# Moving the transposes of a backward pass from TensorE to the DMA crossbar, with the gb factor moved into w2T and the w2 gradient

## The chip, the cores and the metric

The kernel runs on one core of one Trainium2 chip. The metric is the device time of one execution in microseconds (us), the median of several. The kernel before takes 773.13 us (3 runs, 772.19 to 773.19). A profile is one execution, whose span is some 1.75 us shorter than the time of the same run. The batches of runs went to different chips; the kernel before reads 773.2 to 773.6 us in each.

## The reference, cut to what matters

The program computes the forward pass and all gradients of one block: a spectral mixer, then an MLP with a squared ReLU. The change touches the MLP and its gradients.

```python
# S=2048 rows, D=512, F=1792; bf16
h   = layernorm(x1) * (1 + cb) + sb
r   = relu(h @ w1 + b1);  hact = r * r
out = x1 + gb * (hact @ w2 + b2)
# backward, g = grad_out:
#   gb2  = colsum(gb * g)                 gw2 = hact.T @ (gb * g)
#   gh   = 2 r * ((gb * g) @ w2.T)        gb1 = colsum(gh)
#   gw1  = h.T @ gh                       gx1 = layernorm backward of gh @ w1.T, ...
```

## The kernel before

The matmuls here contract over the 128 partitions of their operands, so several operands are needed in the other orientation. The kernel before makes each with TensorE transposes into PSUM, and ScalarE or VectorE copies the result to SBUF. I name the stages after their matmuls: C (`psH`, the first MLP matmul), D (`psO`, the second), E (`psg` and the w2 gradient), F (`psh`, the gradient through w1), G (`psw`, the w1 gradient).

```python
# D, per row tile t: gB = g*gb, transposed; w2 transposed during the first four tiles
nc.vector.tensor_tensor(gbrow, grow, modb[:, 5, :], op=ALU.mult)        # gbrow = gB[:, t, :]
nc.tensor.matmul(gb2_ps, lhsT=K["ones_col"], rhs=gbrow, ...)
for dc in range(4):
    nc.tensor.transpose(pst[:, dc, :], gbrow[:, dc * P:(dc + 1) * P], K["ident"])
nc.scalar.copy(out=gBT[:, :, t * P:(t + 1) * P], in_=pst)
if t < 4: w2T_blocks(t)                                                  # 14 transposes each
# ... E, per block fc of 14: 16 psg matmuls, then
for tg in range(4):                                                      # 16 transposes of rT
    ...
    nc.scalar.copy(out=rnat[:, 4 * tg:4 * tg + 4, :], in_=...)
nc.vector.tensor_tensor(hnat, rnat, rnat, op=ALU.mult)
for t in range(NT):
    nc.tensor.matmul(psw2, lhsT=hnat[:, t, :], rhs=gB[:, t, :], ...)
# ... 4 transposes of w1 into w1T; after the last fc:
nc.sync.dma_start(out5_view, gb1b)       # b1 gradient, "(fc p) -> p fc": 1,792 pieces of 2 bytes
# ... G, two halves of 7 blocks, one buffer ghn:
for j in range(NHALF):                   # 16 transposes of ghT[fc], copies into ghn
    ...
for dc in range(4):
    for cc in range(2):                  # psw1 += h2[:, t].T @ ghn[:, t], 16 matmuls
        ...
```

After G the constants of the spectral mixer are loaded again into the memory of ghT, so these loads cannot start before the last read of ghT.

Of the kernel before, what the change touches and what calls it, by code (L numbers as in the profile page):

```python
# [10 lines left out]
ALU = mybir.AluOpType  # L11
AX = mybir.AxisListType
FP32 = mybir.dt.float32
BF16 = mybir.dt.bfloat16
# [428 lines left out]
def colsum_to_row(tc, K, ps, row16):  # L443
    tc.nc.vector.tensor_copy(row16, ps)
# [3 lines left out]
def kernel(  # L448
# [12 lines left out]
    x1_dram = dram.tile([P, NT, D], BF16, name="x1_dram")  # L461
    xs_dram = dram.tile([P, NT, 2, DF], BF16, name="xs_dram")
    rT_dram = dram.tile([NFC, P, NT * P], BF16, name="rT_dram")
    gx1_dram = dram.tile([P, NT, D], BF16, name="gx1_dram")
# [25 lines left out]
    nc.vector.memset(gsc_acc, 0.0)  # L490
    modb = constp.tile([P, 6, D], BF16, name="modb")
    sbcol = small.tile([P, 4], FP32, name="sbcol")
    cbcol = small.tile([P, 4], FP32, name="cbcol")
# [58 lines left out]
    with tc.tile_pool(name="modps", bufs=2, space=PSUM) as mps:  # L552
# [31 lines left out]
        for jc in range(6):  # L584
# [4 lines left out]
            else:  # L589
                nc.scalar.copy(out=modb[:, jc, :], in_=psb)  # L590
        psc2 = mps.tile([P, 8], FP32, name="modc2_ps", bufs=1)
        for i in range(8):
            nc.tensor.matmul(psc2[:, i:i + 1], lhsT=modrow[:, (12 + i) * P:(13 + i) * P], rhs=one1, start=True, stop=True)
        nc.vector.tensor_copy(sbcol, psc2[:, 0:4])
        nc.vector.tensor_scalar(cbcol, psc2[:, 4:8], 1.0, None, op0=ALU.add)
    build_lf(tc, K, cpool, cg)
# [74 lines left out]
    with tc.tile_pool(name="mlpw1", bufs=1) as mp1, tc.tile_pool(name="rtp", bufs=2) as rtp, \  # L671
# [6 lines left out]
        for fc in range(NFC):  # L678
            rT = rtp.tile([P, NT * P], BF16, name="rT")
            for sc in range(4):  # L680
                psH = psH_pool.tile([P, 4 * P], FP32, name="psH")
                for dc in range(4):
                    nc.tensor.matmul(psH, lhsT=w1[:, dc, fc * P:(fc + 1) * P],  # L683
                                     rhs=h2T[:, dc, sc * 4 * P:(sc + 1) * 4 * P],
                                     start=(dc == 0), stop=(dc == 3))
                nc.scalar.activation(rT[:, sc * 4 * P:(sc + 1) * 4 * P], psH, AF.Relu, bias=b1col[:, fc:fc + 1])  # L686
                nc.vector.tensor_tensor(hactT[fc][:, sc * 4 * P:(sc + 1) * 4 * P],  # L687
                                        rT[:, sc * 4 * P:(sc + 1) * 4 * P],
                                        rT[:, sc * 4 * P:(sc + 1) * 4 * P], op=ALU.mult)
            nc.sync.dma_start(rT_dram[fc, :, :], rT)  # L690
    ph.release()
    pA = tc.alloc_tile_pool(name="pA", bufs=1)
    gB = pA.tile([P, NT, D], BF16, name="gB")
    gBT = pA.tile([P, 4, NT * P], BF16, name="gBT")
    w2T = pA.tile([P, 4, F], BF16, name="w2T")
    rT_pf = {}
    for fc in range(2):
        rT_pf[fc] = pA.tile([P, NT * P], BF16, name="rT_pf", bufs=2)
        nc.sync.dma_start(rT_pf[fc], rT_dram[fc, :, :])
    with tc.tile_pool(name="mlpw2", bufs=1) as mp2:  # L700
# [7 lines left out]
        with tc.tile_pool(name="o2p", bufs=2) as op2, \  # L708
             tc.tile_pool(name="psO", bufs=2, space=PSUM) as psO_pool, \
             tc.tile_pool(name="psG", bufs=1, space=PSUM) as psG_pool, \  # L710
             tc.tile_pool(name="psT3", bufs=2, space=PSUM) as psT3:
            ggb_ps = psG_pool.tile([1, D], FP32, name="ggb_ps")
            gb2_ps = psG_pool.tile([1, D], FP32, name="gb2_ps")
            def w2T_blocks(dc):
                for f0 in range(0, NFC, 4):
                    nb = min(4, NFC - f0)
                    pst = psT3.tile([P, 4 * P], BF16, name="pstw2")
                    for j in range(nb):
                        fc = f0 + j
                        nc.tensor.transpose(pst[:, j * P:(j + 1) * P], w2[:, fc, dc * P:(dc + 1) * P], K["ident"])  # L720
                    nc.scalar.copy(out=w2T[:, dc, f0 * P:(f0 + nb) * P], in_=pst[:, :nb * P])
            for t in range(NT):
# [12 lines left out]
                nc.sync.dma_start(out0_view[:, t, :], o0)  # L735
                grow = op2.tile([P, D], BF16, name="grow")
                nc.sync.dma_start(grow, g_view[:, t, :])
                gprod = op2.tile([P, D], BF16, name="gprod")
                nc.vector.tensor_tensor(gprod, grow, bo, op=ALU.mult)
                nc.tensor.matmul(ggb_ps, lhsT=K["ones_col"], rhs=gprod, start=(t == 0), stop=(t == NT - 1))  # L740
                gbrow = gB[:, t, :]
                nc.vector.tensor_tensor(gbrow, grow, modb[:, 5, :], op=ALU.mult)
                nc.tensor.matmul(gb2_ps, lhsT=K["ones_col"], rhs=gbrow, start=(t == 0), stop=(t == NT - 1))
                pst = psT3.tile([P, 4, P], BF16, name="pstg2")
                for dc in range(4):
                    nc.tensor.transpose(pst[:, dc, :], gbrow[:, dc * P:(dc + 1) * P], K["ident"])
                nc.scalar.copy(out=gBT[:, :, t * P:(t + 1) * P], in_=pst)
                if t < 4:
                    w2T_blocks(t)
            colsum_to_row(tc, K, ggb_ps, ggb_row)  # L750
            colsum_to_row(tc, K, gb2_ps, gb2_row)
            nc.sync.dma_start(out_7[None, :], gb2_row)
# [15 lines left out]
    with tc.tile_pool(name="bwB", bufs=1) as bb:  # L768
        w1n = bb.tile([P, 4, F], BF16, name="w1n")
        nc.sync.dma_start(w1n, w1_view)  # L770
        with tc.tile_pool(name="bwC", bufs=2) as bcp, tc.tile_pool(name="bwC1", bufs=1) as bcp1, \
             tc.tile_pool(name="psGH", bufs=2, space=PSUM) as pgh, \
             tc.tile_pool(name="psRT", bufs=2, space=PSUM) as prt, \
             tc.tile_pool(name="psW2", bufs=1, space=PSUM) as pw2:
            for fc in range(NFC):
# [5 lines left out]
                for sc in range(4):  # L781
                    psg = pgh.tile([P, 4 * P], FP32, name="psg")
                    for dc in range(4):
# [7 lines left out]
                                                   accum_out=gb1acc[:, fc, sc:sc + 1])  # L791
                rnat = bcp1.tile([P, NT, P], BF16, name="rnat")
                for tg in range(4):
                    pst = prt.tile([P, 4 * P], BF16, name="pstr")
                    for j in range(4):
                        t = 4 * tg + j
                        nc.tensor.transpose(pst[:, j * P:(j + 1) * P], rT[:, t * P:(t + 1) * P], K["ident"])  # L797
                    nc.scalar.copy(out=rnat[:, 4 * tg:4 * tg + 4, :], in_=pst.rearrange("p (j f) -> p j f", j=4))  # L798
                hnat = bcp.tile([P, NT, P], BF16, name="hnat", bufs=1)
                nc.vector.tensor_tensor(hnat, rnat, rnat, op=ALU.mult)  # L800
                psw2 = pw2.tile([P, D], FP32, name="psw2")
                for t in range(NT):
                    nc.tensor.matmul(psw2, lhsT=hnat[:, t, :], rhs=gB[:, t, :], start=(t == 0), stop=(t == NT - 1))  # L803
                gw2 = bcp.tile([P, D], BF16, name="gw2", bufs=1)
                nc.scalar.copy(out=gw2, in_=psw2)  # L805
                nc.sync.dma_start(out6_view[:, fc, :], gw2)
                h2_row(fc)
                if fc >= NFC - (NT - NFC):
                    h2_row(fc + (NT - NFC))
                pst = prt.tile([P, 4 * P], BF16, name="pstr")  # L810
                for dc in range(4):
                    nc.tensor.transpose(pst[:, dc * P:(dc + 1) * P], w1n[:, dc, fc * P:(fc + 1) * P], K["ident"])
                nc.vector.tensor_copy(out=w1T[:, fc, :], in_=pst)
        gb1 = bb.tile([P, NFC], FP32, name="gb1")
# [7 lines left out]
    with tc.tile_pool(name="bwD", bufs=1) as bd:  # L822
# [56 lines left out]
        with tc.tile_pool(name="bwF", bufs=1) as bfp, tc.tile_pool(name="bwF2", bufs=2) as bfq, \  # L879
             tc.tile_pool(name="psTg", bufs=2, space=PSUM) as ptg, \  # L880
             tc.tile_pool(name="psW1", bufs=2, space=PSUM) as pw1:
            NHALF = NFC // 2
            for half in range(2):
                ghn = bfp.tile([P, NT, NHALF * P], BF16, name="ghn")
                for j in range(NHALF):
                    fc = half * NHALF + j
                    for tg in range(4):
                        pst = ptg.tile([P, 4 * P], BF16, name="pstg")
                        for jj in range(4):
                            t = 4 * tg + jj  # L890
                            nc.tensor.transpose(pst[:, jj * P:(jj + 1) * P], ghT[fc][:, t * P:(t + 1) * P], K["ident"])  # L891
                        if (j * 4 + tg) % 2 == 0:
                            nc.vector.tensor_copy(out=ghn[:, 4 * tg:4 * tg + 4, j * P:(j + 1) * P],  # L893
                                                  in_=pst.rearrange("p (j f) -> p j f", j=4))
                        else:
                            nc.scalar.copy(out=ghn[:, 4 * tg:4 * tg + 4, j * P:(j + 1) * P],  # L896
                                           in_=pst.rearrange("p (j f) -> p j f", j=4))
                for dc in range(4):
# [139 lines left out]
```

## Time and profile before

In all views PE is TensorE, PEld its weight loads, DVE VectorE, ACT ScalarE, POOL GpSimd and SPq SyncE's DMA queue; PEclk is the granted clock of TensorE as a share of full speed, and "issue" means that the engine waited for nothing that the profile shows.

The head of the page of the kernel before, and two of its costliest groups of instructions (line, engine, operation, output<-input, shapes, count | busy us, mean ns | idle us of the engine before them and what ended it):

```profile
span 770.4 us, 9001 instructions
## 1 busy us (share of the span) xinstructions
PE 576.6 (75%) x3190; PEld 278.1 (36%) x3190; DVE 445.3 (58%) x1126; ACT 251.4 (33%) x404; POOL 48.6 (6%) x138
...
L798 ACT COPY rnat<-pstr 128x512 bf16<-128x512 bf16 x56 | 29.9, 587 | 11.7 <-PE pstr L797 9.7
...
L891 PE MATMUL pstg<-ident,ghT 128*128 128x128 bf16 x224 | 21.0, 242 | 7.7 <-DVE ghn L893 4.0
```

No engine is busy throughout, so the stages have to be read one by one. The windows view of the same profile gives, for a stretch in us, its length and each engine's busy time in it. The stretches are C, D, E, F and then G in three parts: up to the first copy into ghn, up to the last transpose of ghT, up to the last psw matmul.

```profile
core 0: us, PE busy (x) PEld busy (x) DVE busy (x) ACT busy (x) POOL busy (x), PEclk, DMA share, GB/s
167.10:227.60 60.50, 55.35 (x233) 23.16 (x233) 33.36 (x88) 38.37 (x56) 0.00 (x0) 0.91 0.52 189
227.60:308.30 80.70, 71.14 (x382) 29.41 (x382) 39.20 (x94) 18.61 (x35) 0.00 (x0) 0.95 0.30 97
308.30:424.20 115.90, 114.80 (x693) 55.98 (x693) 59.35 (x139) 35.95 (x67) 0.00 (x0) 0.99 0.25 87
424.20:503.40 79.20, 71.18 (x296) 24.37 (x295) 58.65 (x167) 10.88 (x19) 0.00 (x0) 0.94 0.35 99
503.40:529.80 26.40, 10.45 (x29) 2.43 (x28) 18.59 (x50) 5.86 (x10) 0.00 (x0) 0.61 0.21 70
529.80:581.00 51.20, 46.76 (x364) 30.03 (x364) 14.30 (x32) 18.27 (x32) 0.00 (x0) 0.90 0.06 19
581.00:605.30 24.30, 20.66 (x110) 10.47 (x108) 1.87 (x3) 2.18 (x4) 0.00 (x0) 1.00 0.84 335
```

E is TensorE's: 114.80 of 115.90 us. In the second part of G TensorE is busy for 46.76 of 51.20 us, in part with transposes; in the third part the DMA moves 335 GB/s. Lines of the timeline (start, duration, engine, line, operation, and in brackets how long the engine had waited and for what) show the edges:

```profile
272.27 0.23 PEld L746 LDWEIGHTS <-gB 128*128 128x128 bf16 x4 [0.23 <-issue]
...
447.52 0.43 DVE L865 TENSOR_TENSOR gx1row<-v2b,grow_b 128x512 bf16<-128x512 bf16 x1 [8.10 <-DMA grow_b<-in_grad_out_dram]
...
529.81 0.58 ACT L896 COPY ghn<-pstg 128x512 bf16<-128x512 bf16 x1 [1.93 <-DMA out_dram<-gwm]
...
580.69 0.38 PE L891 MATMUL pstg<-ident,ghT 128*128 128x128 bf16 x4
...
581.11 0.33 SPq L918 DMA_DIRECT2D CdB_reload<-CdB_dram  x1
```

Four transposes load in 0.23 us, so each takes 57 ns of TensorE's stream: far less than the 242 ns listed for one in G. (The Trainium skill, "TensorE: Matmul & The Clock Gate", Part 4: PE-mode transpose, reports some 275 ns in a kernel's context. The mean of 242 ns in G is near it, but as occupancy of the stream this trace shows 57 ns.) The copies into ghn begin at 529.81, when the space of stage F is free, and the reloads at 581.11, when the last ghT transpose is done. At 447.52 VectorE has waited 8.1 us in F for a load of 128 KB.

### The profile page before, as it was taken

What the parts mean: (1) busy time and instruction counts of PE and PEld (TensorE: products, weight loads), DVE (VectorE), ACT (ScalarE), POOL (GpSimd) and SP (SyncE); (2) the same over time, 40 slices, a digit from 0 to 9 for tenths busy, and PEclk for the clock granted to TensorE, in tenths of its full rate; (3) what the DMA queues carried; (4) which work ended last, traced back from release to release, by engine and by line L of the source; (5) the groups of instructions that cost most, each with busy time, mean ns of one, the idle gap of its engine ahead of it and who ended that gap; (6) DMA issues with size and microseconds to landing.
All of it is one profiled execution on the core that took longest, in us unless ns stands there. A gap on an engine that the chain in (4) does not pass through costs nothing. (4 is left out here: it accounts for less than half of the span.)

```text
span 770.4 us, 9001 instructions
## 1 busy us (share of the span) xinstructions
PE 576.6 (75%) x3190; PEld 278.1 (36%) x3190; DVE 445.3 (58%) x1126; ACT 251.4 (33%) x404; POOL 48.6 (6%) x138
## 2 busy tenths in 40 slices
PE   1364997457999995999999879955989369397530
PEld 0221683123444332445444323313555146262100
DVE  7977456655744445544554469983131039649981
ACT  2454546335664111223323201113231045144210
POOL 6531002310000000000000000000000000000000
PEclk9995999858999998999999979975999779799855
DMA  7208964577334231412221252321008780321110
GB/s 300 82 27 321 227 158 139 177 210 254 137 136 137 83 101 56 165 69 76 95 71 42 43 163 83 102 75 43 25 25 328 234 250 1 129 91 42 41 54 27
DMA packets 70528, 92.78 MB, mean 120 GB/s; under 512 B 9938, under 2 KB 62804, under 8 KB 69460
## 3 DMA queue, kind: packets, MB, share of 16 engines
q1 hardware_dynamic: 70484, 92.22, 36.8%
q8 instruction: 25, 0.41, 0.2%
q14 instruction: 19, 0.16, 0.1%
HBM read 51.80 MB, written 40.39 MB: 120 GB/s over the span
## 5 line engine op out<-in xcount | busy, mean ns | idle before, releaser
L787 DVE SCALAR_TENSOR_TENSOR ghT<-rT_pf,twof,psg 128x512 bf16<-128x512 bf16 x56 | 40.7, 745 | 55.8 <-PE psg L784 55.6
L784 PE MATMUL psg<-gBT,w2T 128*128 128x512 bf16 x224 | 60.2, 387 | 1.8 <-ACT gwm L439 1.8
L683 PE MATMUL psH<-h2T,w 128*128 128x512 bf16 x224 | 55.1, 402 | 5.2 <-ACT rT L686 4.4
L843 PE MATMUL psh<-w1T,ghT 128*128 128x512 bf16 x224 | 56.3, 392 | 0.4 <-DVE ghT L787 0.4
L902 PE MATMUL psw<-ghn,h2b 128*128 128x448 bf16 x256 | 52.0, 355 | 3.6 <-DVE gw L909 3.6
L725 PE MATMUL psO<-w,hactT 128*128 128x512 bf16 x224 | 53.5, 379 | 0.8 <-ACT rT L686 0.8
L803 PE MATMUL psw<-gB,hnat 128*128 128x512 bf16 x224 | 50.8, 380 | 0.5 <-DVE hnat L800 0.5
L686 ACT ACTIVATE rT<-psH,b1col 128x512 bf16<-128x512 f32 x56 | 38.4, 687 | 22.1 <-PE psH L683 17.4
L687 DVE TENSOR_TENSOR hactT<-rT 128x512 bf16<-128x512 bf16 x56 | 23.7, 424 | 25.3 <-ACT rT L686 25.2
L683 PEld LDWEIGHTS <-w 128*128 128x128 bf16 x224 | 22.7, 101 | 37.0 <-issue 16.3
L843 PEld LDWEIGHTS <-ghT 128*128 128x128 bf16 x224 | 20.0, 100 | 39.8 <-issue 21.6
L798 ACT COPY rnat<-pstr 128x512 bf16<-128x512 bf16 x56 | 29.9, 587 | 11.7 <-PE pstr L797 9.7
L902 PEld LDWEIGHTS <-h2b 128*128 128x128 bf16 x256 | 24.7, 99 | 24.7 <-issue 4.4
L805 ACT CAST gw<-psw 128x512 bf16<-128x512 f32 x14 | 8.2, 585 | 73.8 <-PE psw L803 68.5
L803 PEld LDWEIGHTS <-hnat 128*128 128x128 bf16 x224 | 20.8, 98 | 29.4 <-DVE hnat L800 6.2
L846 ACT CAST gh<-psh 128x512 bf16<-128x512 f32 x16 | 9.4, 585 | 63.2 <-PE psh L843 63.2
L784 PEld LDWEIGHTS <-w2T 128*128 128x128 bf16 x224 | 21.1, 99 | 23.2 <-issue 6.9
L909 DVE CAST gw<-psw 128x448 bf16<-128x448 f32 x8 | 5.0, 624 | 42.3 <-PE psw L902 25.3
L725 PEld LDWEIGHTS <-hactT 128*128 128x128 bf16 x224 | 20.2, 98 | 24.6 <-issue 4.2
L308 POOL MEMSET AE<- 128x2 bf16 x6 | 0.3, 107 | 453.7 <-PE psw L902 441.5
L730 DVE TENSOR_TENSOR bo<-psO,b2b 128x512 bf16<-128x512 f32 x16 | 11.1, 691 | 27.6 <-PE psO L725 27.6
L891 PE MATMUL pstg<-ident,ghT 128*128 128x128 bf16 x224 | 21.0, 242 | 7.7 <-DVE ghn L893 4.0
(326 smaller groups left out, 1084.4 us busy)
## 6 DMA issues: line engine op xcount, KB each, us to landing
rT_dram<-rT SPq DMA_DIRECT2D x14, 512.0 KB, 2.6
rT_pf<-rT_dram SPq DMA_DIRECT2D x14, 512.0 KB, 3.2
w<-in_B_w_dram SPq DMA_DIRECT2D x2, 1792.0 KB, 8.9
wm<-in_w_mod_dram SPq DMA_DIRECT2D x4, 768.0 KB, 10.0
LF_dram<-LF SPq DMA_DIRECT2D x1, 3072.0 KB, 10.3
LG_dram<-LG SPq DMA_DIRECT2D x1, 3072.0 KB
wmc_pf<-in_w_mod_dram SPq DMA_DIRECT2D x6, 512.0 KB, 10.8
out_dram<-gwm SPq DMA_DIRECT2D x24, 128.0 KB, 1.7
```

The source lines that it names most:

```text
L683: nc.tensor.matmul(psH, lhsT=w1[:, dc, fc * P:(fc + 1) * P], rhs=h2T[:, dc, sc * 4 * P:(sc + 1) * 4 * P], start=(dc == 0), stop=(dc == 3))
L686: nc.scalar.activation(rT[:, sc * 4 * P:(sc + 1) * 4 * P], psH, AF.Relu, bias=b1col[:, fc:fc + 1])
L687: nc.vector.tensor_tensor(hactT[fc][:, sc * 4 * P:(sc + 1) * 4 * P], rT[:, sc * 4 * P:(sc + 1) * 4 * P], rT[:, sc * 4 * P:(sc + 1) * 4 * P ...
L725: nc.tensor.matmul(psO, lhsT=hactT[fc][:, t * P:(t + 1) * P], rhs=w2[:, fc, :], start=(fc == 0), stop=(fc == NFC - 1))
L730: nc.vector.tensor_tensor(bo, psO, b2b, op=ALU.add)
L784: nc.tensor.matmul(psg, lhsT=w2T[:, dc, fc * P:(fc + 1) * P], rhs=gBT[:, dc, sc * 4 * P:(sc + 1) * 4 * P], start=(dc == 0), stop=(dc == 3))
L787: nc.vector.scalar_tensor_tensor(out=ghT[fc][:, sc * 4 * P:(sc + 1) * 4 * P], in0=rT[:, sc * 4 * P:(sc + 1) * 4 * P], scalar=K["twof"], in ...
L798: nc.scalar.copy(out=rnat[:, 4 * tg:4 * tg + 4, :], in_=pst.rearrange("p (j f) -> p j f", j=4))
L803: nc.tensor.matmul(psw2, lhsT=hnat[:, t, :], rhs=gB[:, t, :], start=(t == 0), stop=(t == NT - 1))
L843: nc.tensor.matmul(psh, lhsT=ghT[fc][:, t * P:(t + 1) * P], rhs=w1T[:, fc, :], start=(fc == 0), stop=(fc == NFC - 1))
L891: nc.tensor.transpose(pst[:, jj * P:(jj + 1) * P], ghT[fc][:, t * P:(t + 1) * P], K["ident"])
L902: nc.tensor.matmul(psw, lhsT=h2[:, t, dc * P:(dc + 1) * P], rhs=ghn[:, t, cc * 448:(cc + 1) * 448], start=(t == 0), stop=(t == NT - 1))
```

## The change

The change takes 624 TensorE transposes and their copies out (120 in D, 280 in E, 224 in G). DMA transposes, transfers that transpose what they move (crossbar transposes below), take their place: for g and w2 from DRAM, for hact through a new DRAM copy that C stores, for w1 from DRAM, for ghT from SBUF to SBUF. Since g is now transposed as it lies in DRAM, the factor gb moves into w2T and into the outputs of the w2 and b2 gradients. All transposes are issued by SyncE, one stream. The diff below is cut. Cut out as well are gbcol (gb as columns, four small matmuls) and a second PSUM buffer for the w2 gradient in E.

```diff
@@ C
             nc.sync.dma_start(rT_dram[fc, :, :], rT)
+            nc.sync.dma_start(h_dram[fc, :, :], hactT[fc])
@@ between C and D
+    nc.sync.dma_start(gB, g_view)
+    for t in range(NT):
+        nc.sync.dma_start(gBT[:, :, t * P:(t + 1) * P], g_view[:, t, :], transpose=True)
+    nc.sync.dma_start(w2T, B_w2, transpose=True)
+    for dc in range(4):
+        nc.vector.tensor_scalar(w2T[:, dc, :], w2T[:, dc, :], gbcol[:, dc:dc + 1], None, op0=ALU.mult)
@@ D   (cut: transposes of g and w2 with their copies, loads of g per tile)
@@ E   (cut: transposes of rT and w1 with their copies, w1n, hnat bufs=1, the squaring)
+        nc.sync.dma_start(w1T, B_w1, transpose=True)
+                hnat = bcp.tile([P, NT, P], BF16, name="hnat")
+                nc.sync.dma_start(hnat, h_dram[fc, :, :], transpose=True)
-                nc.scalar.copy(out=gw2, in_=psw2)
+                nc.vector.tensor_tensor(gw2, psw2, modb[:, 5, :], op=ALU.mult)
@@ G   (cut: transposes of ghT with their copies)
+                    nc.sync.dma_start(ghn[:, :, j * P:(j + 1) * P], ghT[fc], transpose=True)
```

More of the change, by code (lines that the diff above doesn't have):

```diff
@@ L462 @@
     xs_dram = dram.tile([P, NT, 2, DF], BF16, name="xs_dram")
+    h_dram = dram.tile([NFC, P, NT * P], BF16, name="h_dram")
     rT_dram = dram.tile([NFC, P, NT * P], BF16, name="rT_dram")
@@ L491 @@
     modb = constp.tile([P, 6, D], BF16, name="modb")
+    gbcol = small.tile([P, 4], FP32, name="gbcol")
     sbcol = small.tile([P, 4], FP32, name="sbcol")
@@ L590 @@
                 nc.scalar.copy(out=modb[:, jc, :], in_=psb)
-        psc2 = mps.tile([P, 8], FP32, name="modc2_ps", bufs=1)
-        for i in range(8):
+        psc2 = mps.tile([P, 12], FP32, name="modc2_ps", bufs=1)
+        for i in range(12):
             nc.tensor.matmul(psc2[:, i:i + 1], lhsT=modrow[:, (12 + i) * P:(13 + i) * P], rhs=one1, start=True, stop=True)
         nc.vector.tensor_copy(sbcol, psc2[:, 0:4])
+        nc.vector.tensor_copy(gbcol, psc2[:, 8:12])
         nc.vector.tensor_scalar(cbcol, psc2[:, 4:8], 1.0, None, op0=ALU.add)
@@ L709 @@
              tc.tile_pool(name="psO", bufs=2, space=PSUM) as psO_pool, \
-             tc.tile_pool(name="psG", bufs=1, space=PSUM) as psG_pool, \
-             tc.tile_pool(name="psT3", bufs=2, space=PSUM) as psT3:
+             tc.tile_pool(name="psG", bufs=1, space=PSUM) as psG_pool:
             ggb_ps = psG_pool.tile([1, D], FP32, name="ggb_ps")
             gb2_ps = psG_pool.tile([1, D], FP32, name="gb2_ps")
-            def w2T_blocks(dc):
-                for f0 in range(0, NFC, 4):
-                    nb = min(4, NFC - f0)
-                    pst = psT3.tile([P, 4 * P], BF16, name="pstw2")
-                    for j in range(nb):
-                        fc = f0 + j
-                        nc.tensor.transpose(pst[:, j * P:(j + 1) * P], w2[:, fc, dc * P:(dc + 1) * P], K["ident"])
-                    nc.scalar.copy(out=w2T[:, dc, f0 * P:(f0 + nb) * P], in_=pst[:, :nb * P])
             for t in range(NT):
@@ L735 @@
                 nc.sync.dma_start(out0_view[:, t, :], o0)
-                grow = op2.tile([P, D], BF16, name="grow")
-                nc.sync.dma_start(grow, g_view[:, t, :])
                 gprod = op2.tile([P, D], BF16, name="gprod")
-                nc.vector.tensor_tensor(gprod, grow, bo, op=ALU.mult)
+                nc.vector.tensor_tensor(gprod, gB[:, t, :], bo, op=ALU.mult)
                 nc.tensor.matmul(ggb_ps, lhsT=K["ones_col"], rhs=gprod, start=(t == 0), stop=(t == NT - 1))
-                gbrow = gB[:, t, :]
-                nc.vector.tensor_tensor(gbrow, grow, modb[:, 5, :], op=ALU.mult)
-                nc.tensor.matmul(gb2_ps, lhsT=K["ones_col"], rhs=gbrow, start=(t == 0), stop=(t == NT - 1))
-                pst = psT3.tile([P, 4, P], BF16, name="pstg2")
-                for dc in range(4):
-                    nc.tensor.transpose(pst[:, dc, :], gbrow[:, dc * P:(dc + 1) * P], K["ident"])
-                nc.scalar.copy(out=gBT[:, :, t * P:(t + 1) * P], in_=pst)
-                if t < 4:
-                    w2T_blocks(t)
+                nc.tensor.matmul(gb2_ps, lhsT=K["ones_col"], rhs=gB[:, t, :], start=(t == 0), stop=(t == NT - 1))
             colsum_to_row(tc, K, ggb_ps, ggb_row)
-            colsum_to_row(tc, K, gb2_ps, gb2_row)
+            nc.vector.tensor_tensor(gb2_row, gb2_ps, modb[0:1, 5, :], op=ALU.mult)
             nc.sync.dma_start(out_7[None, :], gb2_row)
@@ L768 @@
     with tc.tile_pool(name="bwB", bufs=1) as bb:
-        w1n = bb.tile([P, 4, F], BF16, name="w1n")
-        nc.sync.dma_start(w1n, w1_view)
-        with tc.tile_pool(name="bwC", bufs=2) as bcp, tc.tile_pool(name="bwC1", bufs=1) as bcp1, \
+        nc.sync.dma_start(w1T, B_w1, transpose=True)
+        with tc.tile_pool(name="bwC", bufs=2) as bcp, \
              tc.tile_pool(name="psGH", bufs=2, space=PSUM) as pgh, \
-             tc.tile_pool(name="psRT", bufs=2, space=PSUM) as prt, \
-             tc.tile_pool(name="psW2", bufs=1, space=PSUM) as pw2:
+             tc.tile_pool(name="psW2", bufs=2, space=PSUM) as pw2:
             for fc in range(NFC):
@@ L791 @@
                                                    accum_out=gb1acc[:, fc, sc:sc + 1])
-                rnat = bcp1.tile([P, NT, P], BF16, name="rnat")
-                for tg in range(4):
-                    pst = prt.tile([P, 4 * P], BF16, name="pstr")
-                    for j in range(4):
-                        t = 4 * tg + j
-                        nc.tensor.transpose(pst[:, j * P:(j + 1) * P], rT[:, t * P:(t + 1) * P], K["ident"])
-                    nc.scalar.copy(out=rnat[:, 4 * tg:4 * tg + 4, :], in_=pst.rearrange("p (j f) -> p j f", j=4))
-                hnat = bcp.tile([P, NT, P], BF16, name="hnat", bufs=1)
-                nc.vector.tensor_tensor(hnat, rnat, rnat, op=ALU.mult)
+                hnat = bcp.tile([P, NT, P], BF16, name="hnat")
+                nc.sync.dma_start(hnat, h_dram[fc, :, :], transpose=True)
                 psw2 = pw2.tile([P, D], FP32, name="psw2")
@@ L809 @@
                     h2_row(fc + (NT - NFC))
-                pst = prt.tile([P, 4 * P], BF16, name="pstr")
-                for dc in range(4):
-                    nc.tensor.transpose(pst[:, dc * P:(dc + 1) * P], w1n[:, dc, fc * P:(fc + 1) * P], K["ident"])
-                nc.vector.tensor_copy(out=w1T[:, fc, :], in_=pst)
         gb1 = bb.tile([P, NFC], FP32, name="gb1")
@@ L879 @@
         with tc.tile_pool(name="bwF", bufs=1) as bfp, tc.tile_pool(name="bwF2", bufs=2) as bfq, \
-             tc.tile_pool(name="psTg", bufs=2, space=PSUM) as ptg, \
              tc.tile_pool(name="psW1", bufs=2, space=PSUM) as pw1:
@@ L886 @@
                     fc = half * NHALF + j
-                    for tg in range(4):
-                        pst = ptg.tile([P, 4 * P], BF16, name="pstg")
-                        for jj in range(4):
-                            t = 4 * tg + jj
-                            nc.tensor.transpose(pst[:, jj * P:(jj + 1) * P], ghT[fc][:, t * P:(t + 1) * P], K["ident"])
-                        if (j * 4 + tg) % 2 == 0:
-                            nc.vector.tensor_copy(out=ghn[:, 4 * tg:4 * tg + 4, j * P:(j + 1) * P],
-                                                  in_=pst.rearrange("p (j f) -> p j f", j=4))
-                        else:
-                            nc.scalar.copy(out=ghn[:, 4 * tg:4 * tg + 4, j * P:(j + 1) * P],
-                                           in_=pst.rearrange("p (j f) -> p j f", j=4))
+                    nc.sync.dma_start(ghn[:, :, j * P:(j + 1) * P], ghT[fc], transpose=True)
                 for dc in range(4):
```

## The prediction

> **What bounds it now.** One core, 770.4 us span (page, part 1): TensorE 75% busy, VectorE 58%, DMA 37%; no single bound. Stages, from the windows view and the timeline:
>
> - C, first MLP matmul, 166-226 us: TensorE 54.8 of 60 us, with one 4.7 us stall of ScalarE for the store of rT.
> - D, second MLP matmul, 226-296: TensorE 67.6 of 70.
> - E, ghT and w2 gradient, 308-431: TensorE 114 of 116 us; 8.47 us per fc.
> - G, w1 gradient, 505-606. Copies into ghn wait until 529.8 for the DMA out of gwm. From 581 on, when the last ghT transpose is done, reloads of constants (DMA at 250-330 GB/s) set the pace to 622. So G's critical part is 529.6 to 581 = 51 us.
>
> **What goes.** 624 TensorE transposes (D 120, E 280, G 224). Four issue in 0.23 us, so one costs 57 ns of the pipe. ScalarE's and VectorE's copies (rnat 29.9, hnat 17.1, ghn 28 us and others) go too, hidden except in G.
>
> - D: 16 x 0.24 + 56 x 0.06 = 7 us of TensorE.
> - E: 32 matmuls x 0.216 us = 6.9 us per fc instead of 8.47: 14 x 1.5 = 21 us. VectorE needs about 4.8 us per fc, so TensorE stays the bound.
>
> **What comes.** The Trainium skill ("DMA: Bandwidth & Descriptors", Latency and other measured facts) states 261 GB/s for a DMA transpose with a non-contiguous middle dimension; this trace has none to compare. As an estimate, a 512 KB transpose takes 2.0 us (plain 512 KB DMAs here land in 2.6-3.2 us).
>
> - C: 14 stores of h (7.3 MB) and the 1.8 MB w1T transpose join a queue already at 193 GB/s; rT has only two buffers. About +6 us.
> - D: gB (2 MB), 16 gBT transposes, w2T and rT_pf are released only after MLP1 (rT_pf now issues at 230.2) and sit ahead of the x1row loads on the one SP queue: 6.8 MB, 25-35 us. TensorE can run some 5 to 8 tiles ahead, then waits. Estimate +5 to +12 us, which eats the 7 us saved. D net about +2.
> - E: per fc one 512 KB transpose, one 512 KB rT load and 128 KB out in 6.9 us (about 170 GB/s): hidden, hnat has two buffers.
> - G: ghn has one buffer, so each half waits for 7 transposes: 7 x 2.0 + 2 = 16 us, exposed twice, plus 21-22 us of matmuls of half 0: 54 us against 51. About +3. Each extra microsecond per transpose costs 14 us here.
>
> **Sum.** +6 +2 -21 +3 = -10; some additions may be hidden, so about -13. **Predicted 760 us, 8 in 10 between 735 and 790.** Chances: faster by over 2% 0.44, within 2% 0.39, slower by over 2% 0.17.
>
> **What would show it.** E: fc period 6.9-7.2 us, TensorE over 95% busy. D: VectorE's o waiting for x1row loads between 240 and 265 us; TensorE gap there. G: psw waiting for DMA ghn<-ghT, twice about 16 us, TensorE idle. C: rT waiting for stores longer than 4.7 us. A 512 KB transpose: 1.8-2.3 us apart in the issues.
>
> **What would make it wrong.** Transposes near 130 GB/s: G +28 us, D +10, result about 790 or more. Transposes at 350 GB/s, or x1row loads scheduled between the transposes: D and G both gain, about 740.

## The result, and the profile after

The changed kernel takes 779.29 us (4 runs, 778.57 to 780.90), the kernel before 773.16 us in the same rounds. The ratio is 1.0082, with a 95% interval of 1.0062 to 1.0102. Ratios here and below are the mean time of one kernel's runs over that of the other's of the same rounds, so not quite the ratio of the medians quoted. The sign is against the forecast of 760 us.

The page after, head and one group:

```profile
span 776.8 us, 7601 instructions
...
PE 529.5 (68%) x2533; PEld 243.1 (31%) x2570; DVE 422.8 (54%) x1073; ACT 180.1 (23%) x274; POOL 48.7 (6%) x138
...
L869 PE MATMUL psw<-ghn,h2b 128*128 128x448 bf16 x256 | 53.9, 374 | 35.9 <-DMA ghn<-ghT 29.9
```

TensorE has 47 us less work (a little less in truth: this trace lacks 37 matmul records, 2,533 against 2,570 weight loads), and the span is longer. The same seven stretches of the windows view (after: the third edge of G is the end of the last crossbar transpose of ghT):

```profile
core 0: us, PE busy (x) PEld busy (x) DVE busy (x) ACT busy (x) POOL busy (x), PEclk, DMA share, GB/s
166.30:233.20 66.90, 56.10 (x219) 22.90 (x224) 33.51 (x88) 38.17 (x56) 0.00 (x0) 0.87 0.85 300
233.20:316.80 83.60, 62.54 (x257) 23.70 (x263) 37.07 (x82) 1.76 (x3) 0.00 (x0) 0.90 0.55 150
316.80:415.20 98.40, 97.93 (x439) 44.09 (x448) 51.54 (x127) 0.00 (x0) 0.00 (x0) 0.98 0.63 158
415.20:495.00 79.80, 65.60 (x263) 22.13 (x267) 57.38 (x164) 8.79 (x15) 0.00 (x0) 0.91 0.41 98
495.00:523.15 28.15, 9.90 (x21) 1.88 (x19) 18.76 (x50) 5.86 (x10) 0.00 (x0) 0.60 0.19 65
523.15:583.70 60.55, 30.55 (x144) 14.64 (x145) 2.50 (x4) 2.66 (x5) 0.00 (x0) 0.79 0.70 137
583.70:609.90 26.20, 23.00 (x112) 11.36 (x112) 1.88 (x3) 1.60 (x3) 0.00 (x0) 0.93 0.79 311
```

| stage | before, us | after, us | difference | forecast |
|---|---|---|---|---|
| C | 60.5 | 66.9 | +6.4 | +6 |
| D, with the step to E | 80.7 | 83.6 | +2.9 | +2 |
| E | 115.9 | 98.4 | -17.5 | -21 |
| F | 79.2 | 79.8 | +0.6 | none given |
| G, to the last psw | 101.9 | 114.9 | +13.0 | +3 |
| all after G | 165.1 | 166.9 | +1.8 | none given |

With C starting 0.8 us earlier these sum to +6.4, the difference of the spans. Within E the period of one block, from the first psg weight load of one block to that of the next, falls from 8.47 to 6.91 us, as forecast (6.9): 1.56 us for 20 transposes, 78 ns each with what surrounds them.

The timeline after: a wait in C, the gap in D, and a last line from F:

```profile
202.29 1.27 ACT L689 ACTIVATE rT<-psH,b1col 128x512 bf16<-128x512 f32 x2 [5.16 <-DMA rT_dram<-rT]
...
235.97 24.16 SPq L701 DMA_TRANSPOSE gBT<-in_grad_out_dram  x16
...
260.18 6.89 SPq L703 DMA_TRANSPOSE w2T<-in_B_w_dram  x1
...
269.20 2.47 DVE L705 TENSOR_SCALAR w2T<-w2T,gbcol 128x1792 bf16<-128x1792 bf16 x4 [12.61 <-DMA w2T<-in_B_w_dram]
274.06 0.43 DVE L735 TENSOR_TENSOR o<-o0m,x1row_o 128x512 bf16<-128x512 bf16 x1 [2.38 <-DMA x1row_o<-x_dram]
...
275.93 0.58 PE L726 MATMUL psO<-w,hactT 128*128 128x512 bf16 x1 [11.22 <-DVE bo L731]
...
437.53 0.43 DVE L843 TENSOR_TENSOR gx1row<-v2b,grow_b 128x512 bf16<-128x512 bf16 x1 [14.28 <-DMA grow_b<-in_grad_out_dram]
```

In C ScalarE waits for the stores of rT twice, 9.6 us in all (once before, 4.7 us). In D the transposes hold SyncE's queue from 236 to 267 us. VectorE, whose instructions run in program order in this trace, waits 12.6 us to scale w2T and 2.4 us more for an x1row load behind the transposes; TensorE then stands still for 11.2 us because its PSUM is not emptied.

In F, at 437.53, VectorE has waited 14.3 us for the load that it had waited 8.1 us for before.

For G, the pieces of the chain of waits (start, us, what) that ended last:

```profile
537.84 4.49 DMA ghn<-ghT
542.46 21.36 PE psw L869 x112
...
576.11 5.18 DMA ghn<-ghT
```

Seven transposes take 523.15 to 542.46 = 19.3 us, 112 of the half's 128 matmuls 21.4 us, and the next seven 563.84 to 583.7 = 19.9 us. Nothing overlaps but the first 16 matmuls of each half.

The view of one tile gives the time that each transpose holds SyncE's queue (min/median/max in ns), here for w1T (1,792 KB), hnat (512 KB from DRAM), ghn (512 KB from SBUF) and gBT (128 KB), and for comparison the plain load of rT (512 KB):

```profile
L760 SPq DMA_TRANSPOSE w1T<-in_B_w_dram x1: 7072/7072/7072, 164.7 to 164.7; - x1
...
L782 SPq DMA_TRANSPOSE hnat<-h_dram x14: 1994/2380/2504, 318.6 to 401.6; - x14
...
L864 SPq DMA_TRANSPOSE ghn<-ghT x14: 1785/2332/3001, 523.2 to 579.0; - x14
...
L701 SPq DMA_TRANSPOSE gBT<-in_grad_out_dram x16: 1203/1264/2944, 236.0 to 258.9; - x16
...
L769 SPq DMA_DIRECT2D rT_pf<-rT_dram x12: 326/327/532, 323.0 to 399.1; - x12
```

And the DMA view gives the median us from issue to landing:

```profile
rT_pf<-rT_dram SPq DMA_DIRECT2D x14, 512.0 KB, 3.5
...
hnat<-h_dram SPq DMA_TRANSPOSE x14, 4.4
ghn<-ghT SPq DMA_TRANSPOSE x14, 4.8
w1T<-in_B_w_dram SPq DMA_TRANSPOSE x1, 10.6
...
out_dram<-gb1b SPq DMA_DIRECT2D x1, 3.5 KB, 16.7
```

So, counted by the time on the queue, 1,792 KB go at 259 GB/s (1,835,008 bytes in 7.07 us; w2T, of the same size, in 6.89), 512 KB at 225 GB/s, 128 KB at 104 GB/s. Counted to its landing w1T goes at 173 GB/s. The forecast's 261 GB/s, from the Trainium skill ("DMA: Bandwidth & Descriptors", Latency and other measured facts), holds on the queue for the two large ones only. Source SBUF or DRAM makes little difference here (2.33 and 2.38 us). A plain load of 512 KB holds the queue for 0.33 us, a transpose of 512 KB for seven times as long: what is issued behind transposes waits for them.

### The profile page after: what moved, and what is told of

The parts are those of the page before. It is cut to its first block, busy times and chain, and to the rows that moved or that the text cites. A ratio compares the mean times of both kernels' runs of the same rounds, so it can differ in the third digit from the quotient of the medians. Undisturbed runs are those within 1.5% of the kernel's fastest.

```text
span 776.8 us, 7601 instructions
## 1 busy us (share of the span) xinstructions
PE 529.5 (68%) x2533; PEld 243.1 (31%) x2570; DVE 422.8 (54%) x1073; ACT 180.1 (23%) x274; POOL 48.7 (6%) x138
## 5 line engine op out<-in xcount | busy, mean ns | idle before, releaser
L869 PE MATMUL psw<-ghn,h2b 128*128 128x448 bf16 x256 | 53.9, 374 | 35.9 <-DMA ghn<-ghT 29.9
L726 PE MATMUL psO<-w,hactT 128*128 128x512 bf16 x219 | 52.3, 384 | 12.9 <-DVE bo L731 11.2
L773 PE MATMUL psg<-gBT,w2T 128*128 128x512 bf16 x218 | 53.9, 387 | 2.1 <-ACT gwm L439 1.8
L785 PE MATMUL psw<-gB,hnat 128*128 128x512 bf16 x221 | 52.4, 379 | 0.2
L776 DVE SCALAR_TENSOR_TENSOR ghT<-rT_pf,twof,psg 128x512 bf16<-128x512 bf16 x56 | 41.8, 748 | 14.3 <-PE psg L773 11.4
L821 PEld LDWEIGHTS <-ghT 128*128 128x128 bf16 x224 | 19.8, 99 | 45.3 <-issue 26.4
L787 DVE TENSOR_TENSOR gw<-psw,modb 128x512 bf16<-128x512 f32 x14 | 9.7, 692 | 35.2 <-PE psw L785 35.2
L317 PE MATMUL psC<-AE,LF 128*128 128x257 bf16 x128 | 16.9, 289 | 12.4 <-ACT AE L333 12.4
L351 PE MATMUL psG<-LG_reload,Zb 128*128 128x256 bf16 x128 | 16.6, 298 | 12.4 <-ACT CSb L360 12.4
L422 ACT CAST gmbc<-gm_psb 128x512 bf16<-128x512 f32 x6 | 3.5, 586 | 88.3 <-PE gm_psb L420 88.3
## 6 DMA issues: line engine op xcount, KB each, us to landing
w<-in_B_w_dram SPq DMA_DIRECT2D x2, 1792.0 KB, 13.3
```

Source lines behind the costliest of these rows:

```text
L317: nc.tensor.matmul(ps[:, o, 0:DF], lhsT=LF[:, y, g, :], rhs=ae[:, ri, 256 * e:256 * e + DF], start=(n == 0), stop=(n == 3))
L351: nc.tensor.matmul(ps[:, ch, :], lhsT=Z[:, g, ri, f0:f0 + P], rhs=LG[:, e + ri, g].rearrange("p r t b -> p (r t b)"), start=(n == 0), stop ...
L726: nc.tensor.matmul(psO, lhsT=hactT[fc][:, t * P:(t + 1) * P], rhs=w2[:, fc, :], start=(fc == 0), stop=(fc == NFC - 1))
L773: nc.tensor.matmul(psg, lhsT=w2T[:, dc, fc * P:(fc + 1) * P], rhs=gBT[:, dc, sc * 4 * P:(sc + 1) * 4 * P], start=(dc == 0), stop=(dc == 3))
L776: nc.vector.scalar_tensor_tensor(out=ghT[fc][:, sc * 4 * P:(sc + 1) * 4 * P], in0=rT[:, sc * 4 * P:(sc + 1) * 4 * P], scalar=K["twof"], in ...
L821: nc.tensor.matmul(psh, lhsT=ghT[fc][:, t * P:(t + 1) * P], rhs=w1T[:, fc, :], start=(fc == 0), stop=(fc == NFC - 1))
```

## The experiments

Theory 1: E's gain is real; the loss is the exposed waits for crossbar transposes in G, queues in C and D, and something in F. The main rival: a crossbar transpose hurts whatever runs beside it, or the parts do not add up. All kernels gave correct results. Stage times in us come from one profile of each and scatter: the kernels of this table that share the changed D read 83.6 to 85.8. The profile of the changed kernel is the lowest of these, so D's loss may be nearer 5 us than 2.9.

| kernel | time, us | ratio to before | C | D | E | F | G | after G |
|---|---|---|---|---|---|---|---|---|
| before | 773.16 | | 60.5 | 80.7 | 115.9 | 79.2 | 101.9 | 165.1 |
| changed | 779.29 | 1.0082 | 66.9 | 83.6 | 98.4 | 79.8 | 114.9 | 166.9 |
| g_te | 770.62 | 0.9969 | 67.1 | 85.4 | 99.2 | 79.7 | 103.4 | 166.8 |
| d_te | 775.33 | 1.0033 | 67.5 | 80.0 | 98.6 | 78.8 | 114.5 | 165.6 |
| x1_act | 780.26 | 1.0094 | 67.6 | 83.6 | 98.7 | 79.7 | 114.0 | 168.1 |
| h_rT | 779.36 | 1.0078 | 61.9 | 84.2 | 100.6 | 80.7 | 115.6 | 167.1 |
| e_only | 767.03 | 0.9913 | 69.3 | 80.6 | 99.2 | 79.5 | 103.6 | 167.2 |
| ghn_pre | 748.66 | 0.9684 | 67.0 | 85.8 | 99.2 | 82.1 | 81.4 | 164.7 |
| d_spread | 776.95 | 1.0039 | 66.8 | 77.2 | 99.8 | 80.8 | 116.0 | 167.3 |
| gb1_act | 783.04 | 1.0120 | 67.4 | 85.4 | 99.0 | 79.5 | 116.7 | 167.5 |
| gb1_late | 780.42 | 1.0114 | 66.7 | 85.8 | 99.1 | 64.3 | 127.8 | 167.3 |
| b_gb1_late | 777.59 | 1.0053 | 60.8 | 79.5 | 116.3 | 68.4 | 117.4 | 166.5 |
| best1 | 741.45 | 0.9584 | 67.0 | 79.3 | 99.0 | 66.6 | 96.6 | 165.4 |
| best2 | 737.92 | 0.9544 | 61.0 | 77.2 | 102.0 | 67.3 | 95.9 | 166.0 |
| gb1_row | 769.82 | 0.9942 | 67.0 | 85.7 | 100.2 | 65.1 | 115.8 | 167.4 |
| b_gb1_row | 765.78 | 0.9897 | 60.3 | 80.1 | 116.9 | 68.2 | 106.2 | 165.5 |
| best3 | 711.38 | 0.9201 | 62.1 | 80.0 | 101.6 | 65.8 | 81.2 | 152.1 |

### g_te: G put back to TensorE

```diff
-                    nc.sync.dma_start(ghn[:, :, j * P:(j + 1) * P], ghT[fc], transpose=True)
+                    # the 16 TensorE transposes and 4 copies of the kernel before
```

> The changed kernel with only the w1 gradient (stage G) put back to TensorE transposes. Theory 1 (the exposed waits for the seven crossbar transposes of each half cost G about 7 us, and the later reload another 4 us): about 768 us, ratio to before 0.992 to 0.996; the stretch from the free ghn buffer to the last transpose falls from 58 back to about 51 us. Rival (crossbar transposes cost nothing themselves, the loss sits in the queue of stages C and D): no change, 778 to 780 us.

Measured: 770.62 us; G is 103.4 us, 11.5 us below the changed kernel. The time lies 2 to 3 us above the expected range, its interval (0.9947 to 0.9990) overlaps the expected ratios, and the rival's 778 to 780 us is ruled out. The stretch from the first copy into ghn (527.0) to the last transpose (576.6) is 50 us, as expected. G's crossbar transposes cost 11 us as they are placed.

### d_te: D put back

```diff
-    nc.sync.dma_start(gB, g_view)          (and the 16 gBT transposes, the w2T transpose, its scaling)
+    # loads, scaling and TensorE transposes in D as before
-                nc.vector.tensor_tensor(gw2, psw2, modb[:, 5, :], op=ALU.mult)
+                nc.vector.tensor_copy(gw2, psw2)
```

> The changed kernel with only stage D put back (g, w2 transposed by TensorE, gb folded into g as before). Theory 1 (the 6.8 MB of loads and transposes ahead of the x1row loads stop TensorE for about 11 us and eat the 7 us that D saves): about 775 to 777 us, and no wait of VectorE's o for x1row loads at 262-275. Rival (D's move gains its 7 us and the loss is elsewhere): about 786 us.

Measured: 775.33 us, D 80.0 us, and no wait for x1row loads. As theory 1 had it: D's move, as placed, costs 3 to 4 us net.

### x1_act: the x1row loads on another queue

```diff
-                nc.sync.dma_start(x1row, x1_dram[:, t, :])
+                nc.scalar.dma_start(x1row, x1_dram[:, t, :])
```

> The changed kernel with the 16 x1row loads of stage D issued on ScalarE's DMA queue instead of SyncE's. Theory 1 (x1row loads stand behind the transposes in one in-order queue): the 12 us gap of TensorE in D goes, about 768 to 770 us. Rival (the DMA engines themselves are full, the order of the queue does not matter): the gap stays at over 8 us, 777 us or more.

Measured: 780.26 us, no gain. But the rival's reason is not shown either. The timeline of this kernel:

```profile
271.06 2.47 DVE L705 TENSOR_SCALAR w2T<-w2T,gbcol 128x1792 bf16<-128x1792 bf16 x4 [12.74 <-DMA w2T<-in_B_w_dram]
275.06 0.42 DVE L735 TENSOR_TENSOR o<-o0m,x1row_o 128x512 bf16<-128x512 bf16 x1 [1.53 <-DMA out_dram<-o]
...
276.94 0.59 PE L726 MATMUL psO<-w,hactT 128*128 128x512 bf16 x1 [10.49 <-DVE bo L731]
```

The wait for x1row is gone, and the gap stays: VectorE's first wait is for w2T itself, 12.7 us. My theory named the last of several waits. This run is also a warning about reading one releaser as the cause.

### d_spread: the same transposes, spread over D

```diff
-    for t in range(NT):                                    # before D
-        nc.sync.dma_start(gBT[:, :, t * P:(t + 1) * P], g_view[:, t, :], transpose=True)
+                nc.sync.dma_start(gBT[:, :, t * P:(t + 1) * P], ...)   # in D's loop over t
+                if t == 7:  nc.sync.dma_start(w2T, B_w2, transpose=True)
+                if t >= 12: # scale block t-12 of w2T
```

> The changed kernel with the 16 gBT transposes issued one per row tile of stage D's loop, the w2T transpose in its middle and the scaling of w2T at its end; nothing added or removed. Theory 1 (D's gap of 11 us is the in-order queue and VectorE's in-order stream behind w2T): D plus the step to E falls from 83.6 to 73-76 us, total 768 to 772 us. Rival (transposes beside D's loads slow them): D stays above 80 us.

Measured: D falls from 83.6 to 77.2 us, short of the 73 to 76 expected; some waits of up to 4 us for w2T and x1row remain. The total of 776.95 us is above the expected range, with an interval (0.9997 to 1.0081) too wide to say how much of the 6 us came through. The gap in D is thus mostly one of placement, not of transposing.

### h_rT: no store of h

```diff
-            nc.sync.dma_start(h_dram[fc, :, :], hactT[fc])
-                nc.sync.dma_start(hnat, h_dram[fc, :, :], transpose=True)
+                nc.sync.dma_start(rnat, rT_dram[fc, :, :], transpose=True)
+                nc.vector.tensor_tensor(hnat, rnat, rnat, op=ALU.mult)
```

> The changed kernel without the store of h: the crossbar transposes the stored rT, and VectorE squares it (1.2 us per fc, as before). Theory 1 (stage C's extra 5.5 us come from the 7.3 MB of h stores on a queue that rT's two buffers wait for): C back to about 62-63 us, E unchanged at 98-99 us, total about 774 to 775 us. Rival a (C's loss comes from the w1T transpose of 7 us at its start): C stays at 66-67 us and the total at 779 us. Rival b (E has no slack for VectorE): E grows to over 103 us.

Measured: C goes back from 66.9 to 61.9 us (60.5 before), so most of C's loss is the 7.3 MB of h stores and not the w1T transpose, which is still there. E takes 2.2 us more. The total of 779.36 us did not improve as expected. The profile is of its fastest run (777.12 us); in it D, F and G are 0.6, 0.9 and 0.7 us longer, no more than the scatter, and what else kept the gain away is not settled. Inside the repaired kernel (best2 against best1) the same edit gave 3.5 us.

### e_only: only the E part of the change

```diff
 # the changed kernel with both edits, g_te and d_te
```

> The kernel before with only the E part of the change: h stored and transposed on the way back, w1 transposed by DMA; stages D and G as before. Theory 1 (the parts add up: E gives about 17 us, C takes about 6): 762 to 767 us, E 98-100 us long. Rival (the parts overlap, and what E gives is lost wherever the next wait is): 770 us or more.

Measured: 767.03 us, at the upper edge of the range, ratio 0.9913 (0.9878 to 0.9949). The parts add up: 779.29 less the 8.7 us of g_te and the 4.0 us of d_te would be 766.6.

### ghn_pre: the same 14 transposes of ghT, issued earlier

```diff
+    bfp = tc.alloc_tile_pool(name="bwF", bufs=2)            # before F, not after it
+    GSZ, GOF = (4, 3, 4, 3), (0, 4, 7, 11)                 # four groups of blocks in two buffers
 ...
                 nc.sync.dma_start(gx1_dram[:, t, :], gx1row)
+                if t % 2 == 1 and t < 14: ghn_load(...)     # one transpose per two row tiles of F
 ...
-            for half in range(2):
+            for gi in range(4):                             # matmuls of 512 or 384 columns
```

> The changed kernel with ghn split into four groups of 4, 3, 4 and 3 blocks in two buffers that are allocated before stage F, so that the first seven crossbar transposes run under F and the other seven under the matmuls of the w1 gradient. The transposes are the same 14, of the same 512 KB. Theory 1 (G lost because of the exposed waits, not because a crossbar transpose is slow): the time from the end of F to the last psw matmul falls from 115 to 75-90 us, total 740 to 755 us. Rival (the crossbar's traffic itself slows what it runs beside): F grows by 10 us or more and the total stays over 770 us.

Measured: 748.66 us, ratio 0.9684 (0.9658 to 0.9709), faster than both kernels. The transposes are no faster; this is the line of this kernel's tile view:

```profile
L807 SPq DMA_TRANSPOSE ghn<-ghT x14: 1857/2329/3122, 439.3 to 555.2; - x14
```

And these are lines of its timeline:

```profile
466.91 2.95 SPq L807 DMA_TRANSPOSE ghn<-ghT  x1
...
503.19 0.82 PE L878 MATMUL psw<-ghn,h2b 128*128 128x512 bf16 x3 [0.30 <-DVE gn L839]
...
537.62 1.95 SPq L807 DMA_TRANSPOSE ghn<-ghT  x1
```

The median is 2,329 ns as before, seven of them run under F, which grows by only 2.3 us, and the psw matmuls start right after F at 503.19. G falls from 114.9 to 81.4 us. So G's loss was exposure, one buffer whose space was still taken by F, and not a slow transpose. F's 2.3 us are, in this one profile, all that the seven transposes cost their neighbour.

### gb1_act, gb1_late and b_gb1_late: the store in front of F

In F the wait for grow_b was longer after the change (14.3 against 8.1 us). In front of that load stands the store of the b1 gradient, 3.5 KB in 2-byte pieces, which takes 16.7 us from issue to landing. First, the other queue:

```diff
-            nc.sync.dma_start(out5_view, gb1b)
+            nc.scalar.dma_start(out5_view, gb1b)
```

> The changed kernel with the store of the b1 gradient (3.5 KB in 2-byte pieces, 16.7 us from issue to landing) on ScalarE's DMA queue. Theory 1 (part of E's gain is given back at F's start, where the first grow_b load stands behind this store): the 14 us wait of VectorE for grow_b falls below 5 us and F shortens by 5 to 10 us, total 769 to 774 us. Rival (the DMA engines work the small pieces off either way, on whichever queue): the wait and the total unchanged.

Measured: 783.04 us, no better than the changed kernel, and the wait stays:

```profile
440.65 0.43 DVE L843 TENSOR_TENSOR gx1row<-v2b,grow_b 128x512 bf16<-128x512 bf16 x1 [13.19 <-DMA grow_b<-in_grad_out_dram]
```

The queue is not what matters. Next, the time: the store is held back to the end of F, in the changed kernel and in the one before.

```diff
-        nc.vector.tensor_copy(gb1b, gb1);  nc.sync.dma_start(out5_view, gb1b)       # end of E
+            nc.vector.tensor_tensor(late, rb[:, NT - 1:NT], rb[:, NT - 1:NT], op=ALU.is_equal)   # 1.0
+            nc.vector.tensor_scalar(gb1b, gb1, late, None, op0=ALU.mult)            # end of F
+            nc.sync.dma_start(out5_view, gb1b)
```

> The changed kernel with the store of the b1 gradient held back until stage F's last row tile (its cast is made to depend on that tile's sum). Theory 1 (this 3.5 KB store in 2-byte pieces occupies the DMA engines, whichever queue it is on, and keeps F's first grow_b load waiting, so part of E's gain is given back in F): VectorE's wait for grow_b falls from 14 us to under 6 us and F from 79.8 to 70-74 us; the total may gain less, since the store now runs beside the gwm stores: 768 to 778 us. Rival (the three wmc loads of 512 KB keep grow_b waiting): wait and F unchanged.

> The same move in the kernel before. Theory 1 (before, E's last matmuls ran to 431 us beside this wait and hid part of it): the wait for grow_b falls from 8.1 us to under 3 us and F shortens by less than in the changed kernel, 2 to 6 us; total 768 to 775 us. Rival (no link): F unchanged at 79 us.

Measured: F falls from 79.8 to 64.3 us in the changed kernel and from 79.2 to 68.4 us in the one before, more than expected in both. The wait in the changed kernel is now:

```profile
427.61 0.43 DVE L839 TENSOR_TENSOR gx1row<-v2b,grow_b 128x512 bf16<-128x512 bf16 x1 [0.45 <-DMA grow_b<-in_grad_out_dram]
```

Without this store in front, the load of grow_b lands at most 5.9 us after its issue instead of 19.7. G grows by 13 and 15 us, since the store now sits there: VectorE waits 14.3 and 13.3 us for stores of gwm. So neither total improves, and both (780.42 and 777.59 us) lie above their ranges. For the explanation the asymmetry counts: E and F together shrink by 195.1 - 178.2 = 16.9 us with the store in place, and by 184.7 - 163.4 = 21.3 us with it out of the way. (The scatter is smaller: g_te, d_te, x1_act and gb1_act, with the same E and F as the changed kernel, read 177.4 to 178.9 us for the two stages.)

### gb1_row and b_gb1_row: the same bytes in 256-byte rows

```diff
-            nc.sync.dma_start(out5_view, gb1b)                       # 1,792 pieces of 2 bytes
+            nc.tensor.transpose(gb1p, gb1b, K["ident"])
+            nc.vector.tensor_copy(gb1r, gb1p)
+            nc.sync.dma_start(out_5.rearrange("(fc p) -> fc p", p=P), gb1r)   # 14 rows of 256 bytes
```

> The changed kernel with the b1 gradient turned by one TensorE transpose and stored as 14 rows of 256 bytes, at the same place. Theory 1 (the two-byte pieces keep F's first loads waiting): F falls from 79.8 to 64-66 us with no growth of G, total 763 to 766 us. Rival (the place, not the pieces): F stays at 79 us.

> The same in the kernel before. Theory 1: F falls from 79.2 to 68-69 us, total 761.5 to 764 us, so the changed kernel would be only 0 to 3 us slower than the one before instead of 6. Rival (no asymmetry): both gain the same and the gap stays at 6 us.

Measured, over 5 rounds: 769.82 and 765.78 us, both above their ranges by 2 to 4 us, with F at 65.1 and 68.2 us as expected. Size of pieces, not place, is what cost F. The gap between the changed kernel and the one before shrinks from 0.82% to 0.45% (0.9942 against 0.9897), so from 6 to about 4 us, short of the 0 to 3 expected; with intervals of 0.2% on each ratio this does not separate the theory from its rival. E and F together differ by 185.1 - 165.3 = 19.8 us now, which speaks for the asymmetry. G of the kernel before grew by 4.3 us with this edit. About 2 us of this lie before the first copy into ghn, where the changed kernel is 1.8 us longer too; neither is explained.

### best1, best2 and best3: repairs together

best1 is ghn_pre, d_spread and gb1_late in one kernel; best2 adds h_rT; best3 takes gb1_row in place of gb1_late and stores the gradient of c (512 pieces of 2 bytes, the last DMA of the kernel) as 4 rows of 256 bytes in the same way.

```diff
-            nc.sync.dma_start(out8_view, gcb)
+            nc.tensor.transpose(gcp, gcb, K["ident"])
+            nc.vector.tensor_copy(gcr, gcp)
+            nc.sync.dma_start(out_8.rearrange("b (dc p) -> (b dc) p", p=P), gcr)
```

> The changed kernel with the prefetched ghn groups, the spread gBT and w2T transposes and the late store of the b1 gradient together. Theory 1 (the three repairs act in different stages and add up): 735 to 745 us, D plus step to E 76-78 us, F end to last psw 80-88 us. Rival (they share one DMA queue and one of them only moves the wait): no better than the prefetched ghn alone, 746 us or more.

> best1 without the store of h: rT is transposed and squared by VectorE. Theory 1 (C gives back 5 us, E costs 2 us for VectorE): 733 to 743 us, 2 to 4 us below best1. Rival (as in the run without the h store, the gain of C is lost again): the same as best1 within 2 us.

> The changed kernel with the prefetched ghn groups, the spread transposes of D, rT transposed in place of a stored h, and the gradients of b1 and c turned on TensorE and stored in 256-byte rows. Theory 1 (the repairs add up; best2 stood at 738, the late store there cost about 13 us in G, and the last store of the kernel, 1 KB in two-byte pieces, holds its end for about 14 us): 710 to 722 us. Rival (something else takes the place of the removed waits): 728 us or more.

Measured: 741.45, 737.92 and 711.38 us. All three totals lie within their ranges, but best1 missed both of its stage ranges (D 79.3 us, G 96.6 us). best3 is 0.9201 (0.9177 to 0.9224) of the kernel before, so the repairs add up; some 14 us of its gain lie after G (152.1 against 166.0 us in best2) and come with the last store, not with the change studied here. The row store of the b1 gradient is no part of that change either, and b_gb1_row gained from it too. A fair comparison is therefore with the kernel before with both stores turned, which was not run: an estimate from b_gb1_row is 765.8 - 14 = 752 us, so some 40 us of best3's gain belong to the DMA transposes in their new places. In best1 and best2 part of G's gain was eaten by the late store (96 against 81 us).

## Why the prediction was right or wrong

The forecast was 760 us and the result 779.29: inside the range of 735 to 790, but with the wrong sign. Of these 19 us G's term holds 10, E's 3.5, the 3 us that "may be hidden" 3, and the stretch after G 1.8. The mechanism was right in C and G, and in E as far as E itself goes; in D it was half right; what E's end does to F was missed.

- **The step that failed: "G: ghn has one buffer, so each half waits for 7 transposes: 7 x 2.0 + 2 = 16 us, exposed twice, plus 21-22 us of matmuls of half 0: 54 us against 51. About +3."** Measured +13.0. The exposed wait is 19.3 and 19.9 us instead of 16, because a 512 KB transpose takes 2.33 us, about 2.5 from one to the next, instead of 2.0, and the last one of the first half lands 4.5 us after its issue. That makes the second part of G 60.6 instead of 54 us. The parts of G before and after it grew by 1.8 and 1.9 us. g_te shows the size (11.5 us of G), ghn_pre that it is exposure: the same transposes at the same speed, moved under F and under matmuls, and G is at 81 us. The forecast's own warning, 14 us for each microsecond per transpose, fits: half a microsecond more makes some 7 us. I took the skill's one rate for 512 KB too, without an allowance per instruction.
- **E, "14 x 1.5 = 21 us": right for TensorE, wrong as time of the kernel.** The period per block fell by 1.56 us, as forecast, but only 17.5 us arrived in E. With the b1 store out of the way E and F shrink by 21.3 us (gb1_late against b_gb1_late), with the rows by 19.8. With the store in place the two stages together give only 16.9 us. Before, E's last matmuls ran to 431 us beside this store and hid part of it; after, E ends earlier, and F's first load waits 14.3 us instead of 8.1. This is a new end of a wait, not a cost of the crossbar. It was visible in the profile before, as the 8.1 us, and I did not ask what E's end would uncover.
- **C, +6:** right, +6.4. h_rT shows that most of it is the h stores.
- **D, +2:** near in size (+2.9; d_te gives back 3.6), in part by luck, since the other kernels with this D read up to 85.8 us, +5. The picture was only half right: I named the x1row loads behind the transposes, and x1_act shows that freeing these loads alone gains nothing. VectorE's scaling of w2T, in order ahead of the rest, waits first. d_spread shows that placement is most of it.
- **The last 3 us** ("some additions may be hidden") had no reading behind them and went the other way: after G the kernel is 1.8 us longer.

What stays open: why h_rT's 5 us in C did not show in its total, how much of d_spread's 6 us did, the 4.3 us by which G grows in b_gb1_row, the 1.8 and 1.9 us in the first and last parts of G and the 1.8 us after it, and the rest of the gap in b_gb1_row.

## What to carry to other kernels

In this kernel a DMA transpose cost little only where its result was needed later than it could be issued (in F 2.3 us for seven). So give it a buffer whose space is free a stage earlier, and spread the issues over the loop that uses them, before counting TensorE's savings as gained. When a stage on the critical path gets shorter, look at what already waits at the start of the next one, because that wait will grow by what the overlap hid. A store in 2-byte pieces can hold up other loads for far longer than its size suggests (here 3.5 KB took 16.7 us, and a 128 KB load beside it 19.7); turn the small tensor first.

## What the Trainium skill lacked or had wrong

- "DMA: Bandwidth & Descriptors", Latency and other measured facts, gives 261 GB/s for a DMA transpose with a non-contiguous middle dimension and some 350 to 400 for a contiguous one, and names no size. Here 1,792 KB went at 259 GB/s, 512 KB at 225 and 128 KB at 104 (7.07, 2.33 and 1.26 us of the queue). An estimate from the first two is 0.4 us per instruction plus 1.9 us per 512 KB; it gives 0.9 us for 128 KB, less than was measured, so the form is not settled, but the entry lacks a term per instruction.
- "Advanced Engine Details and Errata", X-Bar Transpose (TRN2), says that transpose DMAs are as fast as regular ones, 350 to 400 GB/s. Here 512 KB landed 4.4 to 4.8 us after the issue when transposed and 3.5 us when not, and the median rates on the queue were 225 GB/s for 512 KB and 259 and 266 for the two of 1,792 KB (the shortest single one, 512 KB in 1.79 us, is 294).
- "DMA: Bandwidth & Descriptors", Specifications, names 512 bytes as the least transfer for line rate. It gives no time for pieces of 2 bytes: here 3.5 KB in 1,792 pieces took 16.7 us to land and held up loads even on the other queue (wait 13.2 us on the other queue, 0.45 us with the store out of the way).
- "TensorE: Matmul & The Clock Gate", Part 4: PE-mode transpose, gives 275 ns for a transpose in a kernel's context. As a share of TensorE's stream it is 57 ns here (four in 0.23 us), and in E the removal of 20 per block saved 78 ns each (8.47 to 6.91 us per block).
